# Query, key, value, weight and x transfers of the attention stage made as 120 rows and 8 rows

## The chip, the cores and the metric

One core of one Trainium2 chip runs the whole program. The time is device microseconds of one execution; the number before the change is the median of three runs. A profile is one more execution, taken by the hardware profiler.

## The reference

```
scores = q k^T / 8                              # 4 batches, 12 heads, 448 tokens, head size 64, all float32
scores = einsum("bhij,hg->bgij", scores, w_pre) # heads mixed
attn   = exp(scores - max) / (sum + 1e-9)
attn   = einsum("bgij,gh->bhij", attn, w_post)  # heads mixed again
x      = attn v                                 # 1792 tokens x 768
h      = x w_in;  g = h > 0 ? h : exp(h) - 1;  x = g w_out        # w_in 768 x 2048 and w_out are float64
out    = x + gate * relu(x w1[e]) w2[e]  where x . w_skip > 0, else x   # one of 8 experts per token
```

## The kernel before

The program has three stages: attention (the first 350 us or so), the dense layers in float64 weights, and the experts. The order of the instructions on each engine is the order of the code: `attention` runs a loop over 48 units `n` (lines 397 to 468), a dozen for each of the four batches, and the mixtures of the later stages are a generator, `mix`, that the last five units step by `next(mix)` (the steps stand in lines 650 to 697).

A tile `T` is up to 120 queries of one batch; three units make a tile. In a unit, TensorE (PE) does the following: `mix_pre` (line 199, matmuls at L204) mixes the heads of the scores of two groups; `mix_post` (line 249, matmuls at L264: 64 small ones for each group) mixes them again after the softmax; `av` (line 273, L286 and L292) multiplies by the values; `qk` (line 151, L164) makes scores of a tile to come.

`mix_pre` needs the scores with (row, head) on the partitions. This turn is a transfer from memory to memory on the chip, `relayout` (line 185, issued at L196, `d<-s`): it takes 10 rows of the score tile `s` and all 12 heads and writes them on 120 partitions of one of eight tiles `d`. There are 184 of them.

All loads and stores here are issued by SyncE (SP), in order of the code. In each unit SP issues four relayouts, the store of `x` of two heads' pairs (`store`, line 311, L313, into `xT`), and at times queries (`load_q`, line 115, L120), keys (`load_k`, line 122, L124, one transfer per pair of heads, six a batch) and values (`load_v`, line 126, L129, the same). `load_w` (line 526, L528) and `load_x` (line 559, L562) bring the first float64 weights and the first rows of `x` back during the last units. SP's transfers take eight landing counters in turn (`DMAHW0` to `DMAHW7` in the rows of the order below), and each waits until the transfer before it on its counter has landed: at most eight are under way.

Of the kernel before, what the change touches and what calls it, by code (L numbers as in the profile page):

```python
# [8 lines left out]
FP32 = mybir.dt.float32  # L9
# [9 lines left out]
B, H, S, D = 4, 12, 448, 64  # L19
NT, DM, DFF = B * S, H * D, 2048  # L20
NK = DM // 128
# [8 lines left out]
PR = 120  # L30
# [4 lines left out]
ROWS = [(0, 120), (120, 120), (240, 120), (360, 88)]  # L35
WHOLE = S // 128
# [41 lines left out]
    return [(r, BR) for r in range(0, whole, BR)] + [(whole + i * few, few) for i in range(2 if few else 0)]  # L78


def attention(tc, q, k, v, w_pre, w_post, xT, mix, ident):


# [9 lines left out]
    nc = tc.nc  # L93
    with ExitStack() as ctx, ExitStack() as mixing, ExitStack() as scoring:
        pool = lambda name, bufs, ctx=ctx, **kw: ctx.enter_context(tc.tile_pool(name=name, bufs=bufs, **kw))
# [6 lines left out]
        d_p = pool("a_d", 1, mixing)  # L102
        s_p = [pool("a_s0", 1, scoring, side="right"), pool("a_s1", 1, mixing)]
        k_p = pool("a_k", 1, scoring, side="right")
        rk_p = pool("a_rk", 6, scoring, side="right")
        rq_p = pool("a_rq", 2, scoring, side="right")
        q_p = pool("a_q", 3, scoring, side="right")
        ps_f = pool("ps_f", 2, space=PSUM)
# [1 line left out]
        ps_w = pool("ps_w", 4, mixing, space=PSUM, side="right")  # L110

        tiles = [(b, it) for b in range(B) for it in range(len(ROWS))]
        raw_q, raw_k, vt, kt, qt, st, att = {}, {}, {}, {}, {}, {}, {}

        def load_q(T, us=None):
            b, it = tiles[T]
            if T not in raw_q:
                raw_q[T] = rq_p.tile([128, NK, PR], FP32, tag="rq", name="rq")
            for p0, p1 in us or [(0, NK)]:
                nc.sync.dma_start(out=raw_q[T][:, p0:p1], in_=q[b, :, it, p0:p1])  # L120

        def load_k(b, p):
            raw_k[b, p] = rk_p.tile([128, S], FP32, tag="rk", name="rk")
            nc.sync.dma_start(out=raw_k[b, p], in_=k[b, p])  # L124

        def load_v(b, p):

            vt[b, p] = v_p.tile([128, 2 * WHOLE + 1, D], FP32, tag=f"v{p}", name="v")
            nc.sync.dma_start(out=vt[b, p].rearrange("s r d -> s (r d)"), in_=v[b, p])  # L129

        def split_k(b, p, eng):

# [140 lines left out]
        def av(T, u, ps=None):  # L273

            b, it = tiles[T]
            r0, n = ROWS[it]
            whole = None
            if ps is None:
                whole = ps_x.tile([128, 2, 512], FP32, tag="x", name="xp")
                ps = [whole[:, i] for i in range(2)]  # L280
            for i in range(2):
                p = 2 * u + i
                for z in range(2):
                    half = (z + p) % 2
# [10 lines left out]
            for p in (2 * u, 2 * u + 1):  # L295
                if b + 1 < B and it == len(ROWS) - 1:
                    values.append((b + 1, p))
# [12 lines left out]

        def store():
            for to, x in stores:
                nc.sync.dma_start(out=to, in_=x)  # L313
            stores.clear()

        def load_mix():
# [34 lines left out]
        load_k(0, 0)  # L351
        load_k(0, 1)
        load_q(0, [(2, NK)])
        for p in range(2, NK):
            load_k(0, p)
        load_q(1)
        mixing_w = load_mix()
        for t in d_all:
            nc.vector.memset(t[:32], 0.0)
# [7 lines left out]
        values += [(0, p) for p in range(NK)]  # L367
# [29 lines left out]
        for n in range(NP):  # L397
            cur, old = units[n], units[n - 1] if n else ()
            new = units[n + 1] if n + 1 < NP else ()
            T, u = when(n + 5)  # L400
            T1, u1 = when(n + 6)
            T2, u2 = when(n + 7)
            for U in new[1:]:
                relayout(U)
            store()
            if n == NP - 5:
                scoring.close()
            late = n >= NP - 5
            for bp in values[:2] if n else ():
                load_v(*bp)  # L410
            del values[:2 if n else 0]
            if T2 < len(tiles):
                if u2 == 0:
                    load_q(T2)
                if tiles[T2][1] == 0:
                    load_k(tiles[T2][0], 2 * u2)
                    load_k(tiles[T2][0], 2 * u2 + 1)
# [12 lines left out]
            weighted = [av((n - 1) // 3 - 1, (n - 1) % 3)] if n >= 4 else []  # L430
            if T < len(tiles):
                scores.append(qk(T, 2 * u))
            if not late:
                for U in cur[1:]:
                    softmax(U)
            for m in moves:
                m[1](nc.scalar.copy)
                m[0](nc.vector.tensor_copy)
            if late:
                for U in cur[1:]:  # L440
                    softmax(U)
                next(mix)
            keys = (tiles[T1][0], 2 * u1, nc.gpsimd) if T1 < len(tiles) and tiles[T1][1] == 0 else ()
            if n < 3:
                keys = 0, 2 * n, nc.vector
            if keys:
                split_k(*keys)
            if late:
                next(mix)
            norm(cur)  # L450
            for f in weighted:
                f()
            if T < len(tiles):
                scores.append(qk(T, 2 * u + 1))
            for f in scores:
                f()
            if keys:
                split_k(keys[0], keys[1] + 1, keys[2])
            moves = [mix_post(U) for U in old[1:]]
            if late:  # L460
                next(mix)
            for m in moves:
                m[1](nc.scalar.copy)
                m[0](nc.scalar.copy)
            if n == NP - 1:
                av(n // 3 - 1, n % 3)()
            if late:
                next(mix)
# [17 lines left out]
def mixtures(tc, order, xT, w_in, w_out, w_skip, w_gate, w1, w2, ident, gT, wf, wg, x2d, slots, out):  # L486
# [4 lines left out]
    nc = tc.nc  # L491
    with ExitStack() as top:
        def pool(name, bufs, ctx=top, **kw):
            return ctx.enter_context(tc.tile_pool(name=name, bufs=bufs, **kw))
# [25 lines left out]
        with ExitStack() as ctx:  # L520
# [2 lines left out]
            xr_p = pool("xr", 9, ctx, side="right")  # L523
            xh_p = [pool("xh0", NK, ctx, side="right")]

            def load_w(src):
                raw = f64_p.tile([128, DM, 2], I32, tag="f64", name="f64")
                nc.sync.dma_start(out=raw.rearrange("p f t -> p (f t)"), in_=src)  # L528
                return raw

            def narrowing(raw, act=None, dve=None):
# [24 lines left out]

            xs, xraw = {}, {}

            def load_x(tb, kks=range(NK)):
                for kk in kks:  # L560
                    xraw[tb, kk] = xr_p.tile([128, S], FP32, tag="xr", name="xr")
                    nc.sync.dma_start(out=xraw[tb, kk], in_=xT[tb][kk])  # L562

            def high_x(tb, kk):
                xs[tb, kk] = xh_p[tb].tile([128, 2, S], FP32R, tag="xh", name="xh")
# [9 lines left out]
                for kk in kks:  # L575
                    low_x(tb, kk)

            def load_w_in(fc):
                return load_w(w_in[fc])

            def load_w_out(fc):
                return load_w(w_out[fc])
# [64 lines left out]

            raws[0] = load_w_in(0)  # L650
            yield
            yield
            load_x(0, range(2))
            yield
            yield
            load_x(0, range(2, 4))
# [6 lines left out]
            load_x(0, range(4, 6))  # L663
            yield
            high_x(0, 0)
            yield
# [1 line left out]
            yield  # L668
            narrowed[0] = next(step)
            yield  # L670
            raws[1] = load_w_in(1)
            yield
            low_x(0, 0)
            high_x(0, 1)
# [697 lines left out]
```

## Time and profile before

| | |
|---|---|
| median of 3 runs | 998.85 us (996.98 to 999.31) |
| profiled execution, its time and its span | 1004.38 us, 1002.6 us |
| granted TensorE clock, mean | 0.992 |
| PE busy (matmul) | 979.3 us, 98% of the span |
| PE weight loads, VectorE, ScalarE, GpSimd busy | 855.5, 725.1, 553.3, 243.8 us |
| moved by DMA | 200.05 MB, mean 200 GB/s |

Busy times of different engines overlap, so they don't add up to the span. A busy PE is modelled from the starts of its matmuls. The DMA share is the mean busy share of sixteen DMA engines, so 0.63 stands for ten of sixteen. A wait that is put down to "issue" is one for which the profile shows no releaser.

### The profile page before, as it was taken

The page shows a single profiled execution, that of the slowest core. Times are in us where ns is not written, and L with a number is a line of the kernel's source. Part 1 is how long each engine was busy: PE and PEld are TensorE (multiplying, and loading weights), DVE is VectorE, ACT ScalarE, POOL GpSimd, SP SyncE. Part 2 cuts the span into 40 slices and gives each one's busy share as a digit, 9 for nine tenths or more (in the row PEclk, how much of TensorE's full clock was granted, in tenths as well). Part 3 has the DMA queues.
Part 4 walks back from the last instruction along what each step waited for, and adds up shares of the span by engine and source line. Part 5 has one row for each costly group of instructions (what it writes and reads, how often), then busy time and mean ns, then how long its engine had stood idle before and what let it go on. Part 6 is the DMA issues. An engine that isn't in the chain of part 4 may idle for free. (4 is left out here: it accounts for less than half of the span.)

```text
span 1002.6 us, 29974 instructions
## 1 busy us (share of the span) xinstructions
PE 979.3 (98%) x12216; PEld 855.5 (85%) x12216; DVE 725.1 (72%) x1462; ACT 553.3 (55%) x1115; POOL 243.8 (24%) x290
## 2 busy tenths in 40 slices
PE   9999999999998999999999999999999999999997
PEld 4677777777776789998999999999999988889986
DVE  6877677767776786676766478786867748999962
ACT  4887688778776754445545453212122117878760
POOL 2343224225222313223323100100101004452002
PEclk9999999999999999999999999999999999999998
DMA  5674664664557575545666398533433396999800
GB/s 183 223 244 141 204 225 153 201 216 165 184 191 235 171 218 171 165 159 176 213 224 222 121 324 263 168 113 95 126 95 118 115 337 248 393 397 398 343 9 35
DMA packets 129252, 200.05 MB, mean 200 GB/s; under 512 B 32002, under 2 KB 95923, under 8 KB 128856
## 3 DMA queue, kind: packets, MB, share of 16 engines
q1 hardware_dynamic: 126824, 191.60, 56.8%
q0 software_dynamic: 2240, 6.51, 1.8%
q8 instruction: 97, 1.59, 0.7%
q14 instruction: 43, 0.35, 0.1%
q10 hardware_dynamic: 48, 0.00, 0.0%
HBM read 122.86 MB, written 37.65 MB: 160 GB/s over the span
## 5 line engine op out<-in xcount | busy, mean ns | idle before, releaser
L916 PE MATMUL o<-w,gh 128*128 128x384 f32 (+2 forms) x1344 | 238.1, 336 | 0.0
L634 PE MATMUL h<-xh,w 128*128 128x448 f32 x1152 | 235.3, 366 | 1.8 <-DVE xh L570 1.4
L916 PEld LDWEIGHTS o<-w,gh 128*128 128x128 f32 x1344 | 232.0, 188 | 2.0
L634 PEld LDWEIGHTS h<-xh,w 128*128 128x128 f32 x1152 | 215.7, 188 | 20.4 <-DVE xh L570 2.1
L212 DVE TENSOR_REDUCE nmx<-c 128x1 f32<-128x448 f32 x184 | 102.4, 617 | 51.0 <-PE c L204 50.9
L264 PEld LDWEIGHTS f<-kr,e 64*64 64x64 f32 x5888 | 104.4, 134 | 37.3 <-issue 24.1
L225 ACT ACTIVATE e<-c,nmx 128x448 f32<-128x448 f32 x184 | 114.3, 632 | 25.3 <-DVE nmx L212 25.2
L245 POOL TENSOR_SCALAR kr<-kpost,rs 128x60 f32<-128x60 f32 x184 | 79.8, 456 | 189.2 <-DVE rs L240 90.0
L803 DVE SCALAR_TENSOR_TENSOR junk<-x,wrow 128x768 f32<-128x768 f32 x117 | 111.8, 955 | 18.2 <-ACT x L946 15.8
L1084 DVE TENSOR_TENSOR wlo<-w1t,whi 128x1536 fp32r<-128x1536 f32 x64 | 111.0, 1752 | 14.0 <-ACT whi L1082 13.7
L264 PE MATMUL f<-kr,e 64*64 64x60 f32 (+1 forms) x5888 | 106.9, 218 | 4.4 <-issue 3.3
L551 POOL TENSOR_TENSOR wf<-a,p 128x768 f32<-128x768 f32 x32 | 66.1, 2064 | 181.2 <-DVE p L549 139.6
L1082 ACT CAST whi<-w1t 128x1536 fp32r<-128x1536 f32 x64 | 93.9, 1484 | 19.9 <-PE ph L1111 10.5
L788 ACT CAST gh<-gr 128x512 fp32r<-128x512 f32 x56 | 35.0, 624 | 97.7 <-PE o L916 35.5
L204 PE MATMUL c<-d,kpre_low 64*64 64x448 f32 x368 | 84.7, 545 | 0.7 <-DMA d<-s 0.7
L204 PE MATMUL c<-d,kpre_up 60*64 60x448 f32 x368 | 82.2, 545 | 0.0
L270 ACT COPY at<-f 128x420 f32<-128x420 f32 (+1 forms) x136 | 65.4, 516 | 28.7 <-PE f L264 27.9
L292 PE MATMUL xp<-at,v 128*64 128x120 f32 (+1 forms) x1152 | 68.7, 268 | 2.8 <-issue 2.6
L168 ACT ACTIVATE s<-qk 120x448 f32<-120x448 f32 x96 | 52.1, 548 | 30.0 <-PE qk L164 19.5
L851 POOL DMA_INDIRECT slots<-pairs,si x14 | 18.8, 1346 | 204.3 <-DVE si L850 156.2
L164 PE MATMUL qk<-k,qq 64*120 64x448 f32 x504 | 67.0, 389 | 0.6 <-ACT e L225 0.2
L292 PEld LDWEIGHTS xp<-at,v 128*64 128x64 f32 x1152 | 57.4, 140 | 10.5 <-issue 9.2
(189 smaller groups left out, 1329.1 us busy)
## 6 DMA issues: line engine op xcount, KB each, us to landing
w1t<-in_moe_w_dram SPq DMA_DIRECT2D x64, 768.0 KB
d<-s SPq DMA_DIRECT2D x176, 210.0 KB
gT<-g SPq DMA_DIRECT2D x64, 224.0 KB
f<-in_moe_w_in_dram SPq DMA_DIRECT2D x16, 768.0 KB
f<-in_moe_w_out_dram SPq DMA_DIRECT2D x16, 768.0 KB
gr<-gT SPq DMA_DIRECT2D x48, 256.0 KB
rq<-in_q_dram SPq DMA_DIRECT2D x15, 360.0 KB
rk<-in_k_dram SPq DMA_DIRECT2D x24, 224.0 KB
```

Source lines behind the costliest of these rows:

```text
L164: nc.tensor.matmul(out=ps[:PR, :S], lhsT=qt[T, p // 2][rows, a, p % 2, :], rhs=kt[b, p][rows, z, :], start=(i == 0), stop=(i == 2))
L204: nc.tensor.matmul(out=ps[j * UP:(j + 1) * UP, :S], lhsT=kpre_up[UP:UP + HP, :] if z else kpre_low, rhs=d[z, j])
L212: nc.vector.tensor_reduce(out=t, in_=c, op=ALU.max, axis=AX.X, negate=True)
L225: nc.scalar.activation(out=e, in_=c, func=ACTF.Exp, bias=t, accum_out=sms[0][:, k + i:k + i + 1])
L245: nc.gpsimd.tensor_scalar(out=kr, in0=kposts[z], scalar1=rs[:, 2 * i + z:2 * i + z + 1], scalar2=None, op0=ALU.mult)
L264: nc.tensor.matmul(out=ps[to, heads, z, :], lhsT=e[rows, keys * JW:(keys + 1) * JW], rhs=kr[rows, first * HR:(first + n) * HR])
L292: nc.tensor.matmul(out=ps[i][z * 64:(z + 1) * 64, :n], lhsT=vt[b, p][:, jc * 2 + z, :], rhs=att[T][:, jc * H + ORDER.index(2 * p + z), :n] ...
L634: nc.tensor.matmul(out=ps, lhsT=w[:, a, kk, :], rhs=xs[tb, kk][:, z, :], start=(kk == 0 and a + z == 0), stop=(kk == NK - 1 and a == 1))
L803: nc.vector.scalar_tensor_tensor(out=t[:, o:o + n], in0=x2, scalar=1.0, in1=w, op0=ALU.mult, op1=ALU.mult, accum_out=lg[:, e:e + 1])
L916: mm = nc.tensor.matmul(out=po[c][:, :cols[c].stop - cols[c].start], lhsT=gs[i][fc // GC][:, a, fc % GC, :], rhs=wo[fc][:, z, cols[c]], st ...
L1082: nc.scalar.copy(out=hi, in_=t)
L1084: nc.vector.tensor_tensor(out=lo, in0=t, in1=hi, op=ALU.subtract)
```

## The change

A helper makes one transfer as two: the first 120 of the 128 partitions, and then the last 8. The queries of tiles 2 and on, the keys of batches 1 to 3, all values, all stores of `x`, and the weight and `x` loads of the last units go through it. Keys and values come by pairs of what were single transfers, so that their count stays as it is. The first loads of the program, and everything that is loaded after the attention stage, stay one transfer each. SP's transfers are 70 more in all: 48 for stores, 14 for queries, 6 for rows of `x`, 2 for weights. No other engine's instructions change.

```diff
+def halves_of(nc, out, in_):
+    for rows in (slice(0, PR), slice(PR, 128)):
+        nc.sync.dma_start(out=out[rows], in_=in_[rows])
...
-        rk_p = pool("a_rk", 6, scoring, side="right")
+        rk_p = pool("a_rk", 3, scoring, side="right")
...
-            for p0, p1 in us or [(0, NK)]:
+            for p0, p1 in us or ():
                 nc.sync.dma_start(out=raw_q[T][:, p0:p1], in_=q[b, :, it, p0:p1])
+            if not us:
+                halves_of(nc, raw_q[T], q[b, :, it])
...
-        def load_v(b, p):
-            vt[b, p] = v_p.tile([128, 2 * WHOLE + 1, D], FP32, tag=f"v{p}", name="v")
-            nc.sync.dma_start(out=vt[b, p].rearrange("s r d -> s (r d)"), in_=v[b, p])
+        def load_v(b, u):
+            t = v_p.tile([128, 2, 2 * WHOLE + 1, D], FP32, tag=f"v{u}", name="v")
+            for i in range(2):
+                vt[b, 2 * u + i] = t[:, i]
+            halves_of(nc, t.rearrange("s p r d -> s p (r d)"), v[b, 2 * u:2 * u + 2].rearrange("p s c -> s p c"))
...
             for to, x in stores:
-                nc.sync.dma_start(out=to, in_=x)
+                halves_of(nc, to, x)
...
-            load_x(0, range(2))
+            load_x(0, range(2), True)
```

On SP, in a unit in which values and queries are loaded, the program before has these rows (`xT` is the store of `x`, `v` values, `rq` queries, `d` the relayouts; the brackets hold what each waits for):

```order
L313 DMA xT0_57<-x_2328 128x2x88 [waits DMAHW5_49,DVE_49]
L129 DMA v_2381<-in_v_dram 128x448 [waits DMAHW6_49,PE_49]
L129 DMA v_2383<-in_v_dram 128x448 [waits DMAHW7_49,PE_49]
L120 DMA rq_2385<-in_q_dram 128x720 [waits DMAHW0_49]
L196 DMA d6_160<-s_1875 120x1x448 [waits DMAHW1_49,PE_49]
L196 DMA d7_161<-s_1875 120x1x448 [waits DMAHW2_49,PE_49]
```

and the changed program has these in the same unit (L84 is the helper, L213 the relayout):

```order
L84 DMA xT0_57<-x_2333 120x2x88 [waits DMAHW3_49,DVE_49]
L84 DMA xT0_57<-x_2333 8x2x88 [waits DMAHW4_49]
L84 DMA v_2387<-in_v_dram 120x2x448 [waits DMAHW5_49,PE_49]
L84 DMA v_2387<-in_v_dram 8x2x448 [waits DMAHW6_49]
L84 DMA rq_2390<-in_q_dram 120x720 [waits DMAHW7_49]
L84 DMA rq_2390<-in_q_dram 8x720 [waits DMAHW0_49]
L213 DMA d6_160<-s_1876 120x1x448 [waits DMAHW1_49,PE_49]
L213 DMA d7_161<-s_1876 120x1x448 [waits DMAHW2_49,PE_49]
```

Two more transfers stand ahead of the relayouts, one of the store and one of the queries; the values are two transfers in both.

On SP, where the last units load the first float64 weights (`f64`) and the first rows of `x` (`xr`), the program before has

```order
L528 DMA f64_7117<-in_moe_w_in_dram 128x1536 [waits DMAHW5_49,DMAHW6_49,DMAHW4_49,DMAHW7_49,DMAHW0_49,Pool_49]
L562 DMA xr_7166<-xT0_57 128x448
L562 DMA xr_7168<-xT0_57 128x448
L196 DMA d0_154<-s_6615 120x1x448 [waits PE_49]
L196 DMA d1_155<-s_6615 120x1x448 [waits PE_49]
```

and the changed program

```order
L84 DMA f64_7146<-in_moe_w_in_dram 120x1536 [waits DMAHW3_49,DMAHW2_49,DMAHW4_49,DMAHW1_49,Pool_49]
L84 DMA f64_7146<-in_moe_w_in_dram 8x1536
L84 DMA xr_7196<-xT0_57 120x448
L84 DMA xr_7196<-xT0_57 8x448
L84 DMA xr_7199<-xT0_57 120x448 [waits DMAHW5_49]
L84 DMA xr_7199<-xT0_57 8x448 [waits DMAHW6_49]
L213 DMA d0_154<-s_6641 120x1x448 [waits DMAHW7_49,PE_49]
L213 DMA d1_155<-s_6641 120x1x448 [waits DMAHW0_49,PE_49]
```

Six transfers stand ahead of the two relayouts where there were three.

## Rows read from the trace of the kernel before

**Rows 1.** The page, busy time of each engine over the span.
```profile
PE 979.3 (98%) x12216; PEld 855.5 (85%) x12216; DVE 725.1 (72%) x1462; ACT 553.3 (55%) x1115; POOL 243.8 (24%) x290
```

**Rows 2.** Windows of the attention stage and after: engines, PE clock, DMA share, GB/s.
```profile
0.00:345.00 345.00, 331.89 (x8676) 245.18 (x8678) 245.31 (x552) 259.15 (x679) 107.47 (x218) 0.99 0.59 194
345.00:610.00 265.00, 263.23 (x1379) 244.18 (x1376) 181.68 (x271) 130.70 (x218) 62.88 (x33) 1.00 0.62 203
```

**Rows 3.** Waits of PE, 0 to 345 us: total, times, longest.
```profile
PE f L264 <- issue: 3.3, 2, 2.1
PE xp L292 <- issue: 2.6, 2, 2.2
PE xp L286 <- issue: 2.6, 2, 2.3
...
PE c L204 <- DMA d<-s: 0.7, 3, 0.3
```

**Rows 4.** Timeline of PE around its four longest waits: start, length, matmuls.
```profile
119.75 0.38 PE L286 MATMUL xp<-at,v 64*64 64x88 f32 x6 [2.25 <-issue]
...
198.09 0.74 PE L264 MATMUL f<-kr,e 64*64 64x60 f32 x36
200.90 0.59 PE L264 MATMUL f<-kr,e 64*64 64x60 f32 x26 [2.06 <-issue]
...
315.95 0.42 PE L292 MATMUL xp<-at,v 128*64 128x120 f32 x3 [2.24 <-issue]
...
320.87 0.45 PE L264 MATMUL f<-kr,e 64*64 64x60 f32 x16 [1.21 <-issue]
```

**Rows 5.** The page, one DMA queue: packets, MB, share of sixteen engines.
```profile
q8 instruction: 97, 1.59, 0.7%
```

**Rows 6.** Groups of PE between the last two of these waits, 315.9 to 320.8.
```profile
L264 PE MATMUL f<-kr,e 64*64 64x60 f32 (+1 forms) x108 | 2.0, 218 | 0.0
L204 PE MATMUL c<-d,kpre_low 64*64 64x448 f32 x8 | 1.7, 544 | 0.0
L204 PE MATMUL c<-d,kpre_up 60*64 60x448 f32 x8 | 1.7, 544 | 0.0
L292 PE MATMUL xp<-at,v 128*64 128x120 f32 x3 | 0.4, 282 | 2.2 <-issue 2.2
```

**Rows 7.** Windows before, in and after waits; columns as in rows 2.
```profile
115.00:117.25 2.25, 2.25 (x81) 1.76 (x74) 1.45 (x3) 1.95 (x6) 0.01 (x1) 1.00 0.99 277
117.25:119.75 2.50, 0.24 (x14) 0.07 (x6) 1.94 (x6) 2.24 (x7) 0.00 (x0) 1.00 0.63 201
...
197.00:199.00 2.00, 1.84 (x52) 1.09 (x45) 1.38 (x3) 1.67 (x6) 0.07 (x1) 1.00 0.96 290
...
310.00:312.50 2.50, 2.50 (x90) 1.73 (x84) 1.91 (x5) 1.92 (x6) 1.56 (x4) 1.00 0.98 354
...
316.00:319.00 3.00, 3.00 (x99) 2.13 (x102) 2.03 (x4) 0.93 (x2) 2.26 (x4) 1.00 1.06 260
119.75:125.00 5.25, 5.25 (x105) 4.44 (x106) 1.59 (x3) 1.09 (x2) 1.64 (x4) 0.67 0.49 151
201.00:206.00 5.00, 5.00 (x92) 4.10 (x94) 1.98 (x6) 1.26 (x3) 1.64 (x4) 0.66 0.49 144
52.50:55.00 2.50, 2.50 (x97) 2.18 (x87) 2.36 (x5) 2.46 (x9) 0.00 (x0) 1.00 0.87 315
```

**Rows 8.** Instructions of SP by line: issue time in ns, min/median/max, first and last start.
```profile
L196 SPq DMA_DIRECT2D d<-s x184: 655/777/1657, 14.1 to 321.4; - x184
...
L313 SPq DMA_DIRECT2D xT<-x x48: 359/387/1604, 49.7 to 352.3; - x48
...
L120 SPq DMA_DIRECT2D rq<-in_q_dram x17: 398/448/604, 0.8 to 271.5; - x17
```

**Rows 9.** Timeline: four relayouts on SP, and the matmuls that use them.
```profile
115.73 3.75 SPq L196 DMA_DIRECT2D d<-s  x4
...
131.58 0.57 PE L204 MATMUL c<-d,kpre_low 64*64 64x448 f32 x1
```

More of the change, by code (lines that the diff above doesn't have):

```diff
@@ L112, in attention @@
         tiles = [(b, it) for b in range(B) for it in range(len(ROWS))]
-        raw_q, raw_k, vt, kt, qt, st, att = {}, {}, {}, {}, {}, {}, {}
+        raws, raw_q, raw_k, vt, kt, qt, st, att = {}, {}, {}, {}, {}, {}, {}, {}
         def load_q(T, us=None):
@@ L118, in load_q, with load_k @@
                 raw_q[T] = rq_p.tile([128, NK, PR], FP32, tag="rq", name="rq")
-            for p0, p1 in us or [(0, NK)]:
+            for p0, p1 in us or ():
                 nc.sync.dma_start(out=raw_q[T][:, p0:p1], in_=q[b, :, it, p0:p1])
-        def load_k(b, p):
-            raw_k[b, p] = rk_p.tile([128, S], FP32, tag="rk", name="rk")
-            nc.sync.dma_start(out=raw_k[b, p], in_=k[b, p])
-        def load_v(b, p):
-            vt[b, p] = v_p.tile([128, 2 * WHOLE + 1, D], FP32, tag=f"v{p}", name="v")
-            nc.sync.dma_start(out=vt[b, p].rearrange("s r d -> s (r d)"), in_=v[b, p])
+            if not us:
+                halves_of(nc, raw_q[T], q[b, :, it])
+        def load_k(b, u, ps=()):
+            if (b, 2 * u) not in raw_k:
+                t = rk_p.tile([128, 2, S], FP32, tag="rk", name="rk")
+                for i in range(2):
+                    raw_k[b, 2 * u + i] = t[:, i]
+                raws[b, u] = t
+            for p in ps:
+                nc.sync.dma_start(out=raw_k[b, p], in_=k[b, p])
+            if not ps:
+                halves_of(nc, raws[b, u], k[b, 2 * u:2 * u + 2].rearrange("p s c -> s p c"))
+        def load_v(b, u):
+            t = v_p.tile([128, 2, 2 * WHOLE + 1, D], FP32, tag=f"v{u}", name="v")
+            for i in range(2):
+                vt[b, 2 * u + i] = t[:, i]
+            halves_of(nc, t.rearrange("s p r d -> s p (r d)"), v[b, 2 * u:2 * u + 2].rearrange("p s c -> s p c"))
         def split_k(b, p, eng):
@@ L294, in av @@
                                          stop=(jc == WHOLE - 1))
-            for p in (2 * u, 2 * u + 1):
-                if b + 1 < B and it == len(ROWS) - 1:
-                    values.append((b + 1, p))
+            if b + 1 < B and it == len(ROWS) - 1:
+                values.append((b + 1, u))
             def move():
@@ L350, in attention @@
         load_q(0, [(0, 2)])
-        load_k(0, 0)
-        load_k(0, 1)
+        load_k(0, 0, (0, 1))
         load_q(0, [(2, NK)])
-        for p in range(2, NK):
-            load_k(0, p)
-        load_q(1)
+        for u in range(1, 3):
+            load_k(0, u, (2 * u, 2 * u + 1))
+        load_q(1, [(0, NK)])
         mixing_w = load_mix()
@@ L366, in attention @@
             nc.vector.memset(t, 0.0)
-        values += [(0, p) for p in range(NK)]
+        values += [(0, u) for u in range(3)]
         ps = ps_f.tile([128, 512], FP32, tag="f", name="f")
@@ L408, in attention @@
             late = n >= NP - 5
-            for bp in values[:2] if n else ():
-                load_v(*bp)
-            del values[:2 if n else 0]
+            if n and values:
+                load_v(*values.pop(0))
             if T2 < len(tiles):
@@ L415, in attention @@
                 if tiles[T2][1] == 0:
-                    load_k(tiles[T2][0], 2 * u2)
-                    load_k(tiles[T2][0], 2 * u2 + 1)
+                    load_k(tiles[T2][0], u2)
             if PLAIN <= T < len(tiles):
@@ L524, in mixtures, with load_w @@
             xh_p = [pool("xh0", NK, ctx, side="right")]
-            def load_w(src):
+            def load_w(src, late=False):
                 raw = f64_p.tile([128, DM, 2], I32, tag="f64", name="f64")
-                nc.sync.dma_start(out=raw.rearrange("p f t -> p (f t)"), in_=src)
+                to = raw.rearrange("p f t -> p (f t)")
+                if late:
+                    halves_of(nc, to, src)
+                else:
+                    nc.sync.dma_start(out=to, in_=src)
                 return raw
@@ L557, in mixtures, with load_x @@
             xs, xraw = {}, {}
-            def load_x(tb, kks=range(NK)):
+            def load_x(tb, kks=range(NK), late=False):
                 for kk in kks:
                     xraw[tb, kk] = xr_p.tile([128, S], FP32, tag="xr", name="xr")
-                    nc.sync.dma_start(out=xraw[tb, kk], in_=xT[tb][kk])
+                    if late:
+                        halves_of(nc, xraw[tb, kk], xT[tb][kk])
+                    else:
+                        nc.sync.dma_start(out=xraw[tb, kk], in_=xT[tb][kk])
             def high_x(tb, kk):
@@ L576, in split_x, with load_w_in @@
                     low_x(tb, kk)
-            def load_w_in(fc):
-                return load_w(w_in[fc])
+            def load_w_in(fc, late=False):
+                return load_w(w_in[fc], late)
             def load_w_out(fc):
@@ L646, in elu @@
                 return act, dve
-            raws[0] = load_w_in(0)
+            raws[0] = load_w_in(0, True)
             yield
             yield
-            load_x(0, range(2))
+            load_x(0, range(2), True)
             yield
             yield
-            load_x(0, range(2, 4))
+            load_x(0, range(2, 4), True)
             yield
@@ L662, in mixtures @@
             yield
-            load_x(0, range(4, 6))
+            load_x(0, range(4, 6), True)
             yield
@@ L670, in mixtures @@
             yield
-            raws[1] = load_w_in(1)
+            raws[1] = load_w_in(1, True)
             yield
```

## The prediction

> **What bounds the kernel now.** I read the busy times first: PE is busy for 979.3 us of the span, 98%, and no other engine is above 72% apart from PE's own weight loads [rows 1]. So the question for any edit is how much idle PE time it can touch. All transfers that change lie in the first 350 us; the window of the first 345 us holds 331.89 us of PE against 245 and 259 us of VectorE and ScalarE [rows 2]. About 13 us of PE idle time lie there, and behind it PE runs almost without a gap (263.23 of 265 us), so what PE gains or loses ahead of 345 us reaches the end whole.
>
> Then the waits of PE in that stage [rows 3]. The largest are put down to "issue": 3.3, 2.6 and 2.6 us, 8.5 us in six waits. Waiting for a relayout costs 0.7 us. In the timeline four long ones stand out [rows 4], and the one at 200.90 us shows what they are: PE stops after 36 matmuls of a run of 64 equal ones and goes on 2.06 us later with the other 26, with nothing new to wait for in between. An engine that has its data and stops has no instruction.
>
> That is borne out by a count. One queue carries "instruction" packets, 97 of them [rows 5], and PE has 12216 matmuls and as many weight loads [rows 1]: 24432 / 97 = 252 instructions of PE per packet, which is 17 KB for each (1.59 MB / 97). Between the waits that end at 315.95 and 320.87 PE ran 108 + 8 + 8 + 3 = 127 matmuls [rows 6], with their weight loads 254 instructions: one packet. I read both waits as PE at the end of a packet with the next one not yet there. In the 345 us there are (8676 + 8678) / 252 = 69 packets, one per 5 us, and some 4 to 6 of them come too late.
>
> Last, what the DMA engines do then. While only relayouts are under way the share is 0.63, ten engines of sixteen (the window of the wait that ends at 119.75) [rows 7]: ten rows of the score tile, ten engines. Stores, values, queries and keys have 128 rows and bring the share to about 1. In the two to three microseconds ahead of each long wait the share was 0.99, 0.96, 0.98 and 1.06: every engine was taken. I conclude that the packet stood in line, on its engine, behind such transfers, on one of the six engines that relayouts leave free (with a place among the ten it would be late far more often, since relayouts run all the time). It is no strict rule: 52.5 to 55 us has a share of 0.87 and no wait.
>
> **The change, part by part.**
>
> *What it removes.* A transfer of ten rows takes ten engines and one of 128 rows sixteen; 120 rows are fifteen equal shares of eight, so I take it that they use fifteen engines, and that the 8 rows use eight of the same. One engine of the six then carries no load or store of this stage. If it is the one that fetches PE's instructions, the four long waits go. The price of the waits is 8.5 us [rows 3]. With two of them goes a lower clock: behind the wait at 119.75 the granted clock is 0.67 over 5.25 us, and behind that at 200.90 it is 0.66 over 5 us, with PE busy throughout [rows 7]; the low level is 0.5 of full speed, so 0.33 x 5.25 + 0.34 x 5 = 3.4 us. (The clock kept 1.00 behind the wait at 315.95.) Gross gain 11.9 us. Below it the bound is 0, if the fetch has another engine. I take 80%, 9.5 us: the nearest row for how far PE could go is that of the other engines, at most 259 of 345 us busy [rows 2], so no other bound is met at once, but short waits at packets' ends will remain.
>
> The Trainium skill, in "DMA: Bandwidth & Descriptors", section "Why a DMA increments its semaphore by 16 and not by 1", gives the count of engines as the largest number up to 16 that divides the outer sizes of both sides, on the lowest-numbered engines: 15 for 120 rows, 8 for 8. The trace agrees for relayouts (0.63) and 128 rows (0.99); it does not number the engines.
>
> *What it adds.* 70 issues on SP. A store takes SP 0.387 us and a load of queries 0.448 us [rows 8]; 48 x 0.387 + 14 x 0.448 + 8 x 0.39 = 28 us of SP, spread over 48 units of 345 / 48 = 7.2 us. A unit now costs SP 4 x 0.777 + 0.387 + about 0.8 for two loads = 4.3 us, and 4.7 to 5.1 us with the change, so SP stays ahead. What hides it is the lead of the relayouts: four that SP finished issuing at 119.5 us were used at 131.58 us, 12 us later [rows 9]. Bounds: nothing, or 28 us if every issue delayed PE. I take 0.5 us, near the lower end, since PE waits 0.7 us in all for relayouts today [rows 3].
>
> *What it moves.* The same bytes go through fewer engines: eight engines that also carry relayouts get a ninth row of each transfer. Relayouts already hold those engines most of the time; one row more in nine on the other loads is a few per cent of their work, and the cover is the same lead. Nothing if it holds. The pools for keys and values keep their size, and the order on PE, VectorE, ScalarE and GpSimd is the same.
>
> *The sum.* 1004.4 (the profiled execution) - 9.5 + 0.5 = 995.4 us there. The median of the runs is 5.5 us lower than that execution; I carry the difference of 9.0 us over and get 998.85 - 9.0 = 989.9, say 990 us. The runs without a profile may stall less than the profiled one, which is a reason to keep the range open upward.
>
> **The rivals.**
>
> *The fetch has another engine, or waits for something else: no change.* Six engines come into question by the rows and only one is emptied, and the wait could also be for the memory that all transfers share. Then the gain is 0 and the cost 0.5 to 1 us: about 999.5 us. For it: the trace does not name the engine, and the bytes per second stay. Against it: the sharpest rows are about how many engines are taken, not about rates (the wait at 200.90 follows 290 GB/s, that at 320.87 260 GB/s, and 52.5 to 55 us passed 315 GB/s without a wait [rows 7]).
>
> Two rules of the skill lean to this side: "Runtime: NRT & Kernel Launch", section "Instruction fetch mechanics", says that crossing from one fetched block to the next is mostly hidden, and "DMA: Bandwidth & Descriptors", section "Rules for kernel authors", advises against making one transfer as two over disjoint partitions, since both use the same engines. By them the sum would be 999.5 us. The trace differs from the first: 8.5 us of waits for issue.
>
> *Relayouts come late: slower.* In each unit an issue or two more stand ahead of the relayouts on SP, and a relayout may not start before the eighth transfer ahead of it has landed; that window now holds fewer rows. The place is the last ten units, where eight loads are doubled beside the stores: (10 + 8) x 0.39 = 7 us if all of it reaches PE, 998.85 + 7 = 1006 us, and no fetch wait removed. It decides where the lead falls under the 0.4 to 0.8 us added per unit plus the landing. Against it is the lead of 12 us [rows 9] and the 0.7 us of waits for `d`.
>
> *A part only.* The long waits at 119.75 and 200.90 go and the last two stay, because the loads of `x` that the generator makes later are still single transfers, or the ninth rows give back some of it: about half, 994 us.
>
> **How the numbers follow.** Forecast 0.55 (990 us, own range 985 to 993.5), a part only 0.12, no change 0.21, late relayouts 0.12. Three runs of the kernel lie within 0.23% of each other, so 0.3%, 3 us, is about what can be told from no change. Faster by more than that: 0.55 + 0.12 = 0.67, less a little of the part that ends near 996, 0.66. Within it: the no-change case and a remainder, 0.22. Slower: 0.12. The range starts at 984, a little under the gross gain (998.85 - 11.9 = 987) less the spread of the runs, and reaches to 1002, which takes in the no-change case; what it leaves out is most of the late relayouts and a tail below, some 0.15.
>
> **What would show it right or wrong.** Right: PE's waits for issue in the first 345 us fall from 8.5 to under 2 us, no wait of over 1 us stands inside a run of equal matmuls, the granted clock has no dip at 0.66 between 100 and 300 us, and in that stage the DMA share with loads under way stays under 0.95. Wrong: such waits are as many as before at other places (another engine fetches), or waits of PE on L204 for `d<-s` grow from 0.7 us to several (late relayouts). If the waits go and the time does not, PE was not the bound there, and the idle time of PE on L264 for GpSimd's or ScalarE's results will have grown.

## The result and the profile after

The changed kernel takes 1014.86 us, median of 6 runs (1010.71 to 1022.52). The kernel before takes 999.35 us in 6 runs beside them (996.98 to 1006.62). The ratio is 1.0142, 95% interval 1.0111 to 1.0173: 1.4% slower, clear of the noise, where I forecast 990 us and faster.

The profiled execution of the changed kernel took 1010.71 us, the fastest of its six, and that of the kernel before 1004.38 us, one of its slower ones. So the two traces lie only 6.3 us apart, of 15.5 us between the medians. They show what kind of time is lost and in which stage; the whole size is told by the timed runs alone.

The page of the changed kernel, span, busy times and two DMA queues (queue, kind, packets, MB, share of sixteen engines), answers to [rows 1, 5]:

```profile
span 1009.0 us, 30012 instructions
...
PE 978.7 (97%) x12216; PEld 855.4 (85%) x12216; DVE 724.9 (72%) x1462; ACT 553.2 (55%) x1115; POOL 241.8 (24%) x290
...
q1 hardware_dynamic: 127125, 191.61, 58.2%
...
q8 instruction: 97, 1.59, 0.7%
```

PE's work is the same, 978.7 us against 979.3. The same 191.6 MB of data and the same 97 instruction packets were moved. What is new is idle time of PE. Its windows, as in [rows 2]:

```profile
0.00:345.00 345.00, 325.57 (x8546) 239.98 (x8548) 241.19 (x543) 256.52 (x673) 105.31 (x217) 0.99 0.63 192
345.00:610.00 265.00, 262.70 (x1461) 242.86 (x1458) 177.99 (x263) 130.72 (x219) 64.42 (x34) 1.00 0.61 198
```

In the attention stage PE is busy 6.3 us less than before (325.57 against 331.89). The DMA engines are busy for more of it, 0.63 against 0.59, and yet move less, 192 against 194 GB/s. Dividing the rate by the engines that were busy gives 194 / (16 x 0.59) = 20.6 GB/s per busy engine before and 192 / (16 x 0.63) = 19.0 after. I use this quotient below; by the rounding of its rows it is good to about 0.2. With the unrounded sums of the trace it is 20.5 and 19.1, 7% less.

The stores of x on SP mark the stage's end (issue time in ns, min/median/max; first and last start in us), as in [rows 8]:

```profile
L84 SPq DMA_DIRECT2D xT<-x x96: 317/344/1439, 49.7 to 360.5; - x96
```

The last one starts at 360.5 us, before at 352.3: 8.2 us later. From there to the end it is 1009.0 - 360.5 = 648.5 us, before 1002.6 - 352.3 = 650.3. All that the trace shows as lost is lost in the stage that the change edits.

Waits of PE from 0 to 350 us (total, times, longest), as in [rows 3]. L281 was L264 before, L309 and L303 were L292 and L286, L221 was L204:

```profile
PE f L281 <- issue: 5.6, 8, 1.4
PE xp L309 <- issue: 4.8, 3, 3.1
PE xp L303 <- issue: 3.4, 2, 2.5
PE qk L181 <- issue: 2.4, 2, 1.5
...
PE c L221 <- DMA d<-s: 0.2, 1, 0.2
```

This is the main reading. The waits for issue add up to 16.2 us in 15, before 8.5 in six: 7.7 us more, against a stage that ends 8.2 us later. The wait for relayouts fell from 0.7 to 0.2 us. The longest waits in the timeline of PE, as in [rows 4]:

```profile
119.05 0.80 PE L281 MATMUL f<-kr,e 64*64 64x60 f32 x41 [1.20 <-issue]
...
124.97 0.38 PE L303 MATMUL xp<-at,v 64*64 64x88 f32 x6 [2.52 <-issue]
...
204.51 0.59 PE L281 MATMUL f<-kr,e 64*64 64x60 f32 x26 [1.42 <-issue]
...
323.62 0.42 PE L309 MATMUL xp<-at,v 128*64 128x120 f32 x3 [3.07 <-issue]
```

They are of the kind that I had read before, and three of them stand at the same places of PE's stream: behind matmul 2624 of the program, 4778 (204.51, where again 26 equal matmuls of a run are left to do, as at 200.90 before) and 7947. The matmuls up to the first and the last of these waits (the first number in brackets), in the kernel before and in the changed one:

```profile
0.00:119.74 119.74, 115.24 (x2624) 79.55 (x2624) 86.84 (x199) 89.32 (x233) 35.98 (x78) 1.00 0.61 201
0.00:315.94 315.94, 306.01 (x7947) 224.90 (x7948) 224.68 (x511) 241.77 (x636) 95.28 (x202) 0.99 0.59 195
```

```profile
0.00:124.96 124.96, 116.05 (x2624) 80.28 (x2624) 87.29 (x199) 89.44 (x233) 36.13 (x79) 1.00 0.63 193
0.00:323.61 323.61, 306.03 (x7947) 225.11 (x7948) 225.31 (x511) 242.11 (x636) 95.14 (x202) 0.99 0.62 190
```

In the traces of all eighteen kernels of this document, every wait for issue of 0.15 us or more in this stage, 214 in all, stands on one grid of such places, some 127 matmuls (one packet) or a multiple of that apart. The traces also keep the start and the length of each packet of q8. In this stage a packet is under way for 1.16 us in the mean, and for 1.14 before the change, so it does not move slower. It starts later: from PE's first matmul of one packet to the start of the next packet it takes 1.5 us in the mean against 1.2, and more than 3 us for six packets against three. At each wait of 0.7 us or more, in both traces, PE goes on 1.2 to 1.6 us after its packet has landed. So that PE waits for late packets is shown, and what grew is the time until they start.

The windows ahead of these waits and behind two of them, as in [rows 7]:

```profile
118.50:121.00 2.50, 1.95 (x61) 1.55 (x64) 0.25 (x1) 1.02 (x3) 0.26 (x1) 1.00 0.86 282
...
201.00:203.00 2.00, 2.00 (x52) 1.17 (x45) 1.12 (x3) 1.61 (x4) 0.34 (x1) 1.00 0.72 242
203.00:204.50 1.50, 0.09 (x4) 0.00 (x0) 1.42 (x4) 1.50 (x7) 0.00 (x0) 1.00 0.41 73
...
318.50:321.00 2.50, 2.05 (x66) 1.77 (x59) 1.65 (x4) 2.50 (x9) 0.00 (x0) 1.00 0.93 199
...
125.00:130.00 5.00, 5.00 (x94) 3.92 (x98) 1.59 (x3) 1.09 (x2) 1.36 (x4) 0.66 0.41 118
...
323.60:328.60 5.00, 4.98 (x119) 3.30 (x122) 2.61 (x6) 1.40 (x3) 2.44 (x4) 0.66 0.73 229
```

Ahead of these waits the DMA share is 0.86, 0.72 and 0.93; before the change it was 0.96 to 1.06. That would fit an engine left over while loads run, but it does not show one, since elsewhere in the stage the share still passes 1:

```profile
218.00:220.50 2.50, 2.48 (x92) 2.06 (x86) 2.50 (x6) 2.08 (x8) 0.00 (x0) 1.00 1.02 221
```

The instructions are late in any case. The granted clock dips twice, as before, at 0.66 for 5 us.

### The profile page after: what moved, and what is told of

Read it like the earlier page. It is cut to its first block, busy times and chain, and to the rows that moved or that the text cites. A ratio compares the mean times of both kernels' runs of the same rounds, so it can differ in the third digit from the quotient of the medians.

```text
span 1009.0 us, 30012 instructions
## 1 busy us (share of the span) xinstructions
PE 978.7 (97%) x12216; PEld 855.4 (85%) x12216; DVE 724.9 (72%) x1462; ACT 553.2 (55%) x1115; POOL 241.8 (24%) x290
## 5 line engine op out<-in xcount | busy, mean ns | idle before, releaser
L654 PEld LDWEIGHTS h<-xh,w 128*128 128x128 f32 x1152 | 215.9, 188 | 20.3 <-DVE xh L590 2.2
L281 PEld LDWEIGHTS f<-kr,e 64*64 64x64 f32 x5888 | 106.8, 136 | 39.8 <-issue 26.9
L281 PE MATMUL f<-kr,e 64*64 64x60 f32 (+1 forms) x5888 | 110.0, 219 | 6.3 <-issue 5.6
L1102 ACT CAST whi<-w1t 128x1536 fp32r<-128x1536 f32 x64 | 93.8, 1482 | 20.1 <-PE ph L1131 10.5
L221 PE MATMUL c<-d,kpre_low 64*64 64x448 f32 x368 | 85.2, 551 | 0.6 <-ACT k L152 0.3
L221 PE MATMUL c<-d,kpre_up 60*64 60x448 f32 x368 | 82.8, 552 | 0.0
L309 PE MATMUL xp<-at,v 128*64 128x120 f32 (+1 forms) x1152 | 66.9, 264 | 4.8 <-issue 4.8
L186 DVE TENSOR_SCALAR s<-qk 120x448 f32<-120x448 f32 x96 | 58.4, 623 | 12.9 <-PE qk L181 8.8
```

Source lines behind the costliest of these rows:

```text
L221: nc.tensor.matmul(out=ps[j * UP:(j + 1) * UP, :S], lhsT=kpre_up[UP:UP + HP, :] if z else kpre_low, rhs=d[z, j])
L281: nc.tensor.matmul(out=ps[to, heads, z, :], lhsT=e[rows, keys * JW:(keys + 1) * JW], rhs=kr[rows, first * HR:(first + n) * HR])
L654: nc.tensor.matmul(out=ps, lhsT=w[:, a, kk, :], rhs=xs[tb, kk][:, z, :], start=(kk == 0 and a + z == 0), stop=(kk == NK - 1 and a == 1))
L1102: nc.scalar.copy(out=hi, in_=t)
```

## The experiments

My first theory after the result was the **ninth row**: the 120-row and the 8-row transfer both start at the first engines, so eight engines get nine rows, instruction packets ride on one of these, and stand behind one row more. Rivals: **more issues** on SP, the **stores**, and **slow rows**: a transfer of 120 rows holds its engines for longer per byte, whatever the number of transfers. Each ratio is to the kernel before, timed beside the versions.

**Which split.** Four versions of the helper; the number of transfers is that of the change in all but the third.

```
e1_cols     half = out.shape[1] // 2
            for cols in (slice(0, half), slice(half, 2 * half)):
                nc.sync.dma_start(out=out[:, cols], in_=in_[:, cols])
e2_rows112  for rows in (slice(0, 112), slice(112, 128)):
e3_whole    nc.sync.dma_start(out=out, in_=in_)
e5_rows88   for rows in (slice(0, 88), slice(88, 128)):
```

> Every transfer of the helper is made as two, as in the change, but by columns: both have all 128 rows, so all sixteen engines take eight rows of each, and SP issues the same 70 more. Ninth row (the fetch of PE's instructions runs on one of the first eight engines, which get a ninth row of each transfer): as before, 998 to 1002 us, PE's waits for issue in the first 345 us near 8.5 us. More transfers (70 more on SP, of which eight may be under way, are what costs): as the change, 1011 to 1017 us. Slower rows (120 rows on fifteen engines move slower, row by row, than 128 on sixteen): as before, 998 to 1002 us.

> 112 and 16 rows in place of 120 and 8: all sixteen engines take seven rows and then one, so none gets more than another; 70 more issues, as in the change. Ninth row: as before, 998 to 1002 us. More transfers: 1011 to 1017 us. Slower rows: in between or as the change, 1004 to 1016 us, with a DMA share above 0.59 in the first 345 us, if 112 rows lie as badly as 120.

> Every transfer of the helper is one, of all 128 rows; keys and values stay by pairs, so SP issues 21 fewer than before the change. Ninth row and slower rows: as before, 997 to 1002 us. More transfers: a little faster than before, 993 to 997 us, since the window of eight holds more bytes.

> 88 and 40 rows: eleven engines take eight rows, and the first ten another four, so five engines carry no load or store of this kind. Ninth row: much worse than the change, 1020 to 1040 us, with PE's waits for issue at 25 us or more. Fetch on one of the last five engines (and the change's loss from elsewhere): these waits nearly vanish, and the time is no more than the change's. More transfers: as the change, 1011 to 1017 us. Slower rows: 1010 to 1025 us.

Measured: halves by columns 998.15 us, 0.9970 (0.9944 to 0.9997); 112 and 16 rows 1004.67, 1.0016 (0.9981 to 1.0051); whole 1001.92, 0.9979 (0.9945 to 1.0013); 88 and 40 rows 1018.34, 1.0177 (1.0119 to 1.0234). The kernel before took 1002.76 beside them. The window of the attention stage of e1_cols, and its waits for issue:

```profile
0.00:345.00 345.00, 332.75 (x8725) 246.11 (x8726) 249.57 (x559) 263.68 (x688) 107.53 (x218) 1.00 0.60 197
```

```profile
PE xp L304 <- issue: 2.1, 3, 1.1
PE xp L310 <- issue: 1.7, 2, 1.4
PE f L282 <- issue: 1.7, 4, 0.7
```

With as many issues on SP as in the change, but 128 rows in each transfer, PE waits 5.5 us for issue, the engines move 197 / (16 x 0.60) = 20.5 GB/s each, and the loss is gone. More issues are excluded. So is the loading of keys and values by pairs, which e3_whole keeps. In e5_rows88 the waits are 15.9 us. Its window of the stage, and the one with the highest share of the hundred windows of 2.5 us from 50 to 300 us:

```profile
0.00:345.00 345.00, 325.35 (x8569) 239.66 (x8570) 241.55 (x545) 258.14 (x675) 104.96 (x217) 1.00 0.59 192
112.50:115.00 2.50, 2.50 (x102) 2.27 (x94) 2.40 (x5) 2.42 (x8) 0.00 (x0) 1.00 0.76 209
```

By the Trainium skill's rule for the count of engines, which the prediction cites ("DMA: Bandwidth & Descriptors", section "Why a DMA increments its semaphore by 16 and not by 1"), 88 rows go over eleven engines and 40 over ten, so that five engines would carry no load and ten would carry 12 rows. The trace agrees: the share stays at 0.76 or less, where it reaches 0.99 in the same windows of the changed kernel. By its median it is the slowest of these four; its interval overlaps that of the change. Taking loads off the last engines does not help, and putting more rows on fewer engines hurts, though by this row the engines' rate is 192 / (16 x 0.59) = 20.3.

**A burden on some engines only.** The loads whole, and behind each an extra transfer that nothing waits for, from memory to memory, of 8, 4 or 2 rows and two key pieces each; then of 16, 10 or 8 rows and four pieces. Beside them the change with its stores whole, and halves of 64 rows.

```
+    nc.sync.dma_start(out=out, in_=in_)
+    to, src = EXTRA[0][EXTRA[1] % len(EXTRA[0])], EXTRA[2]
+    EXTRA[1] += 1
+    nc.sync.dma_start(out=to, in_=src)
     ...
+    EXTRA[:] = [[dram.tile([8, 2, S], FP32, name=f"extra{i}") for i in range(16)], 0,
+                v[0, 0:2, 0:8].rearrange("p s c -> s p c")]
f4_loads    -  halves_of(nc, to, x)      +  nc.sync.dma_start(out=to, in_=x)
g1_rows64   for rows in (slice(0, 64), slice(64, 128)):
```

> The version with whole transfers (keys and values by pairs), and behind each of its 91 transfers one more from memory to memory that the computation doesn't use: eight rows of two pieces of 1792 bytes, so two pieces on each engine that takes part, and by its eight rows on eight engines. Ninth row (PE's instructions are fetched through one of the first eight engines, and what is added there makes them late): 1008 to 1020 us, PE's waits for issue in the first 345 us from 10 to 16 us or more. Slower rows (the 120 rows themselves were the cost): 998 to 1004 us, waits near 10 us.

> The same with four rows in place of eight: the same two pieces for each engine that takes part, but on four engines. Ninth row: as with eight rows if the fetch is on one of the first four, 1008 to 1020 us; as without the extra, 998 to 1004 us, if it is on the fifth to the eighth. Slower rows: 998 to 1004 us.

> The same with two rows: two pieces on two engines. Ninth row: 1008 to 1020 us if the fetch is on one of the first two, 998 to 1004 us if not. Slower rows: 998 to 1004 us.

> The change with the stores of x left whole: queries, keys, values, weights and late rows as 120 and 8, so 22 more transfers on SP than before. Ninth row: the loads hold most of the bytes of the ninth rows (by rows of 1792 to 6144 bytes, some 6 of 9 us on such an engine), so most of the loss stays, 1006 to 1014 us; were the 48 extra packets of the stores what makes the fetch wait, 1000 to 1006 us. Slower rows: most of the loss stays, 1006 to 1014 us.

> 64 and 64 rows: sixteen engines take four rows of each, so every engine has eight in all, as in whole transfers, but each transfer touches only one half of the partitions. Slow rows (what costs is where an engine's rows lie: several engines write the same part of the memory at a time, and rows take longer beside relayouts): as slow as the change or slower, 1008 to 1030 us, with PE's waits for issue at 14 us or more and a DMA share of 0.62 or more in the first 345 us. Fewer engines (only transfers on fewer than sixteen engines cost): as with whole transfers, 997 to 1004 us, waits near 10 us.

> Whole transfers, and behind each a transfer from memory to memory that the computation doesn't use: sixteen rows of four pieces of 1792 bytes, so four pieces on every engine, the one that fetches PE's instructions included. Any theory in which work on that engine delays the fetch: waits for issue above the 10 us of whole transfers, 13 us or more, and 1004 to 1015 us. If the time stays at 998 to 1003 us, work of this kind does not delay the fetch, and the extras on eight, four and two engines said nothing of the place.

> The same on ten engines, four pieces each. Fetch on the ninth or tenth engine: as with sixteen, 1004 to 1015 us, and more than with eight. Fetch on the eleventh to sixteenth: as with whole transfers, 997 to 1003 us.

> The same on eight engines, four pieces each (twice the pieces of the run with two). Fetch on one of the first eight: 1004 to 1015 us. Fetch elsewhere: 997 to 1003 us.

Measured, two pieces: 8 rows 1.0024 (1.0005 to 1.0044), 4 rows 1.0014 (0.9991 to 1.0037), 2 rows 0.9984 (0.9951 to 1.0017). Four pieces: 16 rows 1.0059 (1.0026 to 1.0092), 10 rows 1.0031 (0.9997 to 1.0064), 8 rows 1.0032 (1.0004 to 1.0060). The change with whole stores 1013.26 us, 1.0156 (1.0116 to 1.0196); halves of 64 rows 1009.08 us, 1.0076 (1.0042 to 1.0111). The windows of the attention stage of g2_extra16, f4_loads and g1_rows64, one after the other:

```profile
0.00:345.00 345.00, 326.87 (x8566) 240.51 (x8566) 240.55 (x543) 257.38 (x675) 105.48 (x217) 1.00 0.68 220
```

```profile
0.00:345.00 345.00, 327.13 (x8579) 241.41 (x8580) 243.23 (x547) 258.38 (x675) 105.27 (x217) 1.00 0.63 193
```

```profile
0.00:345.00 345.00, 324.40 (x8578) 242.49 (x8579) 243.09 (x547) 257.60 (x675) 105.17 (x217) 1.00 0.63 192
```

Three things follow. The stores are not the cause: with them whole the loss is as large. Extra work on the engines can be a cost in itself: in g2_extra16 the share rises to 0.68 and the rate with it (220 GB/s, 20.2 for each engine), and 0.6% is lost, with these waits of PE in 0 to 360 us:

```profile
PE xp L313 <- issue: 3.7, 3, 1.9
PE f L285 <- issue: 3.6, 5, 1.5
PE c L225 <- DMA d<-s: 3.2, 3, 2.8
PE xp L307 <- issue: 2.4, 3, 1.7
```

Here a relayout came late as well, 3.2 us in all against 0.7 before; in g1_rows64 it is 3.2 us too, in one wait, and in g3_extra10 and g4_extra8 it is 4.2 and 3.8 us. The waits for issue are 10.2 us in g2_extra16, not the 13 or more that I had expected, and 7.1 and 5.7 in the other two. So what the extra work adds there is late relayouts more than late instructions. In f1_extra8 they are 3.9 us, the least of all, at the DMA share of the change:

```profile
0.00:345.00 345.00, 333.31 (x8742) 247.83 (x8744) 249.76 (x561) 265.55 (x691) 107.47 (x218) 1.00 0.63 206
```

How busy the engines are over the whole stage is thus not what sets the time that late packets cost. The extra rows of g4_extra8 lie on eight engines and have twice the bytes of the change's 8 rows of keys and values; they cost 0.3%, not 1.4%. I had meant to find the engine of the instruction packets with this series; 8, 10 and 16 engines do not differ enough for that, and it **stays open**.

**The 120 rows alone.** h1_extra8 keeps every transfer whole and puts behind each load of queries, keys and values an 8-row load into a tile that nobody reads: the ninth row without the 120. h2_kvq splits those same loads into 120 and 8 rows, everything else whole. h3_only120 is h2_kvq without the 8-row transfers of queries and keys, and of values behind the first batch; its rows 120 to 127 hold old values, so that its output is not the reference's and other tokens reach the experts. h4_pieces makes the loads of 128 rows in two to four pieces by columns.

```
h1_extra8   the lines of the extra transfer above, with
+           EXTRA[:] = [[const.tile([128, 2, S], FP32, name=f"extra{i}")[PR:] for i in range(2)], 0,
h2_kvq      stores, weights and late rows:  -  halves_of(nc, to, src)   +  nc.sync.dma_start(out=to, in_=src)
h3_only120  rows = slice(0, 128 if whole else PR)
            nc.sync.dma_start(out=out[rows], in_=in_[rows])
h4_pieces   for i in range(n):
                nc.sync.dma_start(out=out[:, i * w:(i + 1) * w], in_=in_[:, i * w:(i + 1) * w])
```

> Whole transfers, and behind each load of queries, keys and values one more transfer of eight rows of two pieces of 1792 bytes into a tile that nothing reads, on the same last eight partitions as the change's small transfers. Eight small rows (the second transfer, with its ninth row on eight engines, is the cost): 1007 to 1015 us, waits for issue of PE 13 us or more. Slower rows (the 120 rows over fifteen engines are the cost): 997 to 1003 us, waits 10 us or less.

> Of the change only the loads of queries, keys and values as 120 and 8 rows; the stores, the first weights and the late rows of x are whole. Both theories: most of the loss, 1006 to 1013 us. If it is 998 to 1003 us, the loss was in the few weight and x loads at the end of the stage.

> As the run before, with the transfers of 8 rows left out: queries, keys and values are loaded in 120 rows only, into tiles that stay in place, and the last eight rows keep what the first, whole loads put there (so the output isn't the reference's). One engine of sixteen carries no load then, none has a ninth row, and SP issues fewer transfers than before the change. Eight small rows: as with whole transfers, 996 to 1002 us. Slower rows: as slow as with them, 1005 to 1013 us, and rows of loads beside relayouts that take longer than in whole transfers. The engine that is left free being PE's: below 995 us.

> All rows in every transfer, but less of each row: queries in three pieces, keys and values in two, the first weights in four, stores and late rows whole. If what delays the fetch is how long one transfer holds an engine, a little faster than before, 993 to 998 us, and as fast as halves by columns or faster; if it is only the number of bytes under way, as before, 998 to 1003 us.

Measured: h1_extra8 1002.35 us, 1.0017 (0.9981 to 1.0053); h2_kvq 1009.05, 1.0081 (1.0048 to 1.0114); h3_only120 1041.73, 1.0425 (1.0386 to 1.0465); h4_pieces 1001.85, 1.0001 (0.9970 to 1.0031). The windows of h1_extra8, h2_kvq and h3_only120:

```profile
0.00:345.00 345.00, 329.55 (x8694) 244.04 (x8696) 246.38 (x553) 260.46 (x681) 107.68 (x218) 1.00 0.61 197
```

```profile
0.00:345.00 345.00, 325.13 (x8470) 239.81 (x8470) 239.92 (x541) 255.08 (x671) 103.48 (x215) 0.98 0.61 191
```

```profile
0.00:345.00 345.00, 326.19 (x8648) 242.37 (x8648) 244.79 (x549) 258.10 (x675) 105.59 (x218) 1.00 0.62 192
```

The ninth row without the 120 costs nothing that can be told, and the rate is 197 / (16 x 0.61) = 20.2. **The theory of the ninth row falls.** The 120 rows with or without the 8 give PE 325.13 and 326.19 us in the window, 19.6 and 19.4 GB/s for each engine, and 15.9 and 13.3 us of waits for issue, against 10.0 in h1_extra8. The total of h3_only120 needs a correction: the end of its attention stage and its span,

```profile
span 1036.1 us, 30303 instructions
```

```profile
L329 SPq DMA_DIRECT2D xT<-x x48: 360/390/699, 49.2 to 354.2; - x48
```

leave 1036.1 - 354.2 = 681.9 us for the rest, against 650.3 before, with more instructions, since the experts get other tokens. Without these 31.6 us its median would be 1010.1 us, an estimate that takes the rest as equal in its other executions; h2_kvq took 1009.05. It is a weak one: in its own trace the stage ends only 1.9 us later than before. Between h2_kvq (1.0081) and f4_loads (1.0156) lie only the weights and the late rows of x in two transfers; their intervals lie just apart. So, by the medians, about half of the loss is at queries, keys and values, where it comes with the 120-row loads, and the other half with weights and late rows, where 120 and 8 rows were not tried apart.

The times of single rows, which the trace keeps as well, say the same without the quotient. In the first 345 us a row of 1792 bytes (keys, values, relayouts) takes 82 ns in the mean before the change and 88 after. A row of 6144 bytes (the first weights) takes 309 before, 394 after, 422 in f4_loads, and 301 in h2_kvq, where these loads are whole.

## Why the prediction was wrong

*That late instructions are what PE loses in this stage: right.* The step that carries the whole argument holds, and the grid of places and the landings of the packets show it better than I had: the stage's end moves with the waits for issue (8.5 us and 352.3 us before; 16.2 and 360.5 after; 5.5 and 348.5 in e1_cols). The page has a second queue of instruction packets, q14, which I passed over; the waits follow the landings of q8.

*What it removes: the step that failed.* I let one engine of six be freed and took it that the late packets rode on that one, for a gain of 9.5 us. That an engine was freed is not shown: the share ahead of the long waits fell to 0.93 and less, 15 / 16 being 0.94, but it is 1.02 at 218 us, where my own sign wanted less than 0.95. That the packets rode on it is refuted as far as it was tried: the waits went from 8.5 to 16.2 us, and with five engines without loads (e5_rows88, share at most 0.76 from 50 to 300 us), all but one of the six, they were 15.9 us. That speaks against the step before it as well, that the packets stand on one of the engines that relayouts leave free. I had put 9.5 us of gain on one engine out of six, with no row that singled it out; by that reading alone one in six was the chance. The wait at 204.51 (share 0.72, then 0.41 at 73 GB/s) shows further that a taken engine everywhere is no condition for a late packet.

*What it moves: the term that was left out.* I wrote that the same bytes go through fewer engines, a few per cent more for eight of them, at no cost, because relayouts have a lead of 12 us. For relayouts that was right (their wait is 0.2 us). But the queue that I had just named as the late one, the instruction packets, has no such lead, and I did not price the edit for it. The term that I put at nothing measured 15.5 us by the medians, of which the two traces show 7.7 us as more waits for instructions. Nor did I see that the rows themselves would take longer: not the ninth row (h1_extra8, 1.0017) but the rate of each engine changed, from 20.6 to 19.0 GB/s. Across the runs, transfers of 128 rows give 20.1 to 20.6 with any number of transfers, and ones of 120, 112 or 64 rows 19.0 to 19.6. The rate alone doesn't set the time: 112 and 16 rows, at 194 / (16 x 0.62) = 19.6 by its window, lose nothing that can be told, and 88 and 40 rows lose most at 20.3, with 12 rows on ten engines. What goes with late packets in every trace is the shape of the loads: where all have 128 rows, whole or cut by columns, with extra transfers or without, the waits for issue are 3.9 to 10.2 us (eleven kernels, one profile each); where loads have fewer rows, they are 11.7 to 16.2 us (seven kernels). Why that shape makes packets start late is not shown. At the moment of the fetch the load does matter: over all eighteen traces the mean share in the 1.2 us after PE's first matmul of a packet is 0.42 where the next packet starts within 0.6 us, and 0.78 where it starts after more than 3 us.

The last window that this rests on is that of e2_rows112:

```profile
0.00:345.00 345.00, 328.58 (x8648) 242.89 (x8648) 244.69 (x549) 258.26 (x675) 105.67 (x218) 1.00 0.62 194
```

Why rows of a 120-row load are slower is only argued. The Trainium skill, "DMA: Bandwidth & Descriptors", section "The descriptor swizzle", says that in a transfer to 128 partitions each engine writes one memory port of its own; where rows are dealt in shares of 8 from 120, engines would meet at ports. The rates of 20.6 for whole transfers and 19.0 for 120 and for 64 rows agree with that, the 20.3 of 88 and 40 rows does not, and no run here shows a port. The Trainium skill's rule that the prediction cites from the same page (section "Rules for kernel authors"), against making one transfer as two over disjoint partitions, was the right advice; two halves of 64 rows measured 1.0076, and the price that I put beside it, 999.5 us, was too small.

*What it adds: right.* 70 more issues on SP cost nothing: e1_cols has them too, at 0.9970.

*The clock: wrong.* I had both dips go, 3.4 us; two of 5 us at 0.66 are there, one behind the same place of the stream (matmul 2624) and one behind matmul 7947, where the clock had kept 1.00.

*The rivals.* "No change" fits the runs in its reason, that the fetch has another engine or waits for something else, and was 15 us short. The slower rival, relayouts late, had the sign but not the mechanism: the wait for relayouts fell. (It is seen in g1_rows64 and in g2_extra16, g3_extra10 and g4_extra8, at 3.2 to 4.2 us.) No case of mine held a slower time by more late packets, and that is why the range ended at 1002. The 0.3% that I took for noise was small as well: 25 executions of the kernel before, beside e1_cols, lie between 997.28 and 1011.38 us.

*What stays open:* the engine or resource that holds up the start of PE's instruction packets; why loads of fewer than 128 rows hold it up more; why 88 and 40 rows are as slow as the change or slower, at a higher rate; and the 9.2 us between medians (15.5 less 6.3) that the profiled executions do not show, which I take to be more waits of the same kind, but have not seen.

Of all versions the halves by columns are the fastest, 998.15 us, some 3 us under the kernel before by the ratio (0.9970, 0.9944 to 0.9997), and not told apart from whole transfers (e3_whole, 0.9979). Cutting finer still, in h4_pieces, gives nothing (1.0001), so how long one transfer holds an engine is, by what was expected of that run, not what delays a packet.

## What to carry to other kernels

When an edit changes the shape of transfers, price it for every queue that shares the engines, instructions among them, and not for the data alone: the lead that hides a late relayout hides no late instruction. To see whether an engine waits for instructions, count its instructions up to each wait: here the waits of all kernels stood at the same places of the stream. If a load must be split, split it by columns and keep the 128 rows; splitting by rows was neutral at best and cost up to 1.8% here. And where a mechanism leaves six places open, a forecast that needs one of them deserves one chance in six until a row picks it out.

## What was new about the hardware

A PE that needs nothing but its next instructions stopped for up to 3.1 us at one time (in e3_whole 3.9, in e5_rows88 4.2), in a stage whose DMA engines were busy for about 0.6 of the time. The row of e5_rows88:

```profile
PE xp L309 <- issue: 4.5, 2, 4.2
```

At its waits of 0.7 us or more, before and after the change, it went on 1.2 to 1.6 us after its packet had landed. The bytes of this stage cost 7% more engine time each when the loads had 120 and 8 rows in place of 128 (19.1 against 20.5 GB/s for each engine). And transfers that no one waits for, 26 GB/s over sixteen engines (220 against 194 in the windows), made a kernel bound by TensorE 0.6% slower (g2_extra16).
